# Upper weight parts of the first up projection: seven of eight made on GpSimd instead of ScalarE

## The chip, the cores and the metric

The kernel runs on one core of a Trainium2 chip. The metric is the device time of one execution in microseconds (us). The engines are named as the profile names them: PE is TensorE's matmul (PEld its weight load), DVE is VectorE, ACT is ScalarE, POOL is GpSimd and SP is SyncE, which issues the DMAs here.

## The reference

What is computed is chunked attention with memory tokens, followed by two feed-forward blocks, all in float32:

```python
# attention: 4 x 8 heads, 768 positions, head size 64; chunks of 32 see 16 to the left, 8 to the right, 8 memory keys
scores = scale * np.matmul(q_c, k_full.transpose(0, 1, 3, 2))
a = np.exp(scores - np.max(scores, axis=-1, keepdims=True))
a = a / (np.sum(a, axis=-1, keepdims=True) + 1e-09)
out[:, :, c_start:c_end] = np.matmul(a, v_full)
# x: 3072 tokens x 512
h = x @ w_in                          # w_in 512 x 2048
g = s * np.maximum(h, 0.0) ** 2 + b
x = g @ w_out                         # 2048 x 512
h = x @ w2_in
return (h - np.tanh(h)) @ w2_out
```

The weights arrive in double precision. Each float32 product is made on TensorE from a rounded upper part and a remainder of both factors: three matmuls, upper with upper, remainder with upper, upper with remainder (`three`, L226 to L229). The factor `s` is taken into the first up projection as the product of its weights with `root`, the square root of |s|.

## The kernel before, in words

The tokens are worked in units of 128 (attention) and blocks of 512 (products). The program is written in a fixed order, `manual_schedule`: every engine runs its instructions in the order in which the code emits them. For the first hundred microseconds this order is the table `START`, a list of tokens such as `i5 k0 h5 r6 o5`; each is a letter for a step and a number. Attention of the first units, the preparation of the first up projection's weights and its first tiles are interleaved there.

The weights of the first up projection come in eight pieces n = 0 to 7, each 128 partitions by 1024 values. A piece passes through these tokens:

- `ra`: a DMA of the piece (1 MB) into one of two places (`raw`, L519), issued on SP. Piece n + 2 uses the place of piece n, so its load waits until `l` of piece n has read it. The same places serve the first load for the second up projection (`wl1`).
- `z`: ACT makes the scaled float32 word of the upper half (`scaled`, L234).
- `i`: DVE shifts it in place (`shifted`, L240).
- `o`: DVE fills in the low bits, into `raw` (`filled_in_raw`, L250). It reads two tensors in SBUF.
- `h`: the product of the shifted word with `root`, rounded: the upper part, the first half of `w` (`w1_high`, L541). It reads what `i` made and needs nothing of `o`.
- `l`: DVE makes the remainder from the filled word, `root` and the upper part: the second half of `w` (`w1_low`, L545). It reads two tensors in SBUF.

Beside them stand, for attention unit u: `S` scores on PE, `M` mask and `R` maximum on DVE (L380, L390), `E` eight exponentials on ACT (L398), `D` division: POOL adds 1e-9 to the sums (L411), DVE takes the reciprocal (L412) and multiplies (L413), `T` transposes on PE (L429), `C` copies on ACT, `V` products with the values on PE (L466), `X` and `L` upper part and remainder of the result. For tile t of the up projection: `F` products on PE (L227 to L229), `r` the relu on ACT (L572), `Q` the square, on ACT or on DVE (L586, which reads the product from PSUM and the relu from SBUF), `k` and `K` sums of finished tiles on DVE (L598, two tensors in SBUF). Tiles 2n and 2n + 1 need piece n; three PSUM banks serve the tiles in turn, so that tile t + 3 waits until tile t has been read. `ws1` is the first scaled word for the second up projection, on ACT (L234, `zw`).

Of the kernel before, what the change touches and what calls it, by code (L numbers as in the profile page):

```python
# [98 lines left out]
VALUES_BETWEEN = {  # L99
    0, 2, 6, 8, 10, 11,  # L100
}
HIGH_ON_VECTOR = set()
COPY_ON_VECTOR = set()
PLAIN_EXPONENTIALS = set()

# [36 lines left out]
def tile_chunk_attention_two_ffn(  # L142
# [11 lines left out]
    nc = tc.nc  # L154
# [30 lines left out]
    def new(place, n, dt, name):  # L185
        assert n <= SIZE[place[0]], (place, n)
        if place[0] in "QSRYWV":
            assert place[0] in side["letters"], place
        pool = arena if place[0] in "EZ" else side["of"]
        return pool.tile([P, n], dt, tag=place, name=name)  # L190
# [342 lines left out]

    def w1_high(n):
        w1_w[n] = new(A_W[n], 2048, F32R, "w")
        if n in HIGH_ON_VECTOR:
            nc.vector.tensor_scalar(
                out=w1_w[n][:, 0:1024], in0=w1_z[n], scalar1=root[:, 0:1], scalar2=None, op0=ALU.mult
            )
        else:  # L540
            nc.scalar.activation(out=w1_w[n][:, 0:1024], in_=w1_z[n], func=AF.Copy, scale=root[:, 0:1])  # L541
# [399 lines left out]
    def p2_store_sums(n):  # L941
# [5 lines left out]
        "T": transposes, "C": copies, "V": values, "X": x_high, "L": x_low,  # L947
        "ra": w1_load, "z": w1_scaled, "i": lambda n: shifted(w1_z[n]),
        "o": w1_filled, "h": w1_high, "l": w1_low,
        "G": lambda t: up1_products(t, 0, HB),  # L950
        "F": lambda t: up1_products(t, HB if t < HALVED else 0),
# [266 lines left out]
    for s in range(NQ - 1):  # L1218
        q, p, r = quads2[s], quads2[s - 1] if s else None, quads2[s + 1]
        n, g = q.n, q.g  # L1220
# [202 lines left out]
```

## Time and profile before

| | us |
|---|---|
| median of 3 runs | 1028.87 (1028.59 to 1029.10) |
| the profiled execution, its own time | 1029.12 |
| its span, first to last instruction | 1027.3 |
| PE busy | 1015.4 (99%) |
| DVE busy | 788.6 (77%) |
| ACT busy | 573.2 (56%) |
| POOL busy | 11.3 (1%) |
| granted TensorE clock, mean of the core | 1.000 |

Nearly all of the span is matmuls: the chain of work that ended last is PE for 93%. The shares of DVE and ACT are averages over stages. In the first tenth of the span, where the change lies, both are busy nearly all the time; there the question is which of the engines waits for another, and by how much each piece of work is early.

### The profile page before, as it was taken

The numbers are of one execution on the slowest core, as the hardware profiler recorded it, in microseconds if no ns is written. First come the engines' busy times: TensorE is split into PE (matmuls) and PEld (weight loads), VectorE is DVE, ScalarE is ACT, GpSimd is POOL, SyncE is SP. The second block draws the span as 40 slices with busy tenths as digits, with TensorE's granted clock in tenths as the row PEclk, the third lists the DMA queues.
The fourth block names the chain that finished last, engine by engine and source line by source line (L and its number), as shares of the span: only waits on it lengthen the run. The fifth ranks groups of instructions, "written<-read, shape, count | busy, mean of one in ns | idle before, by whom it ended". The sixth has DMA issues, their size and how long they took to land.

```text
span 1027.3 us, 15607 instructions
## 1 busy us (share of the span) xinstructions
PE 1015.4 (99%) x6112; PEld 842.0 (82%) x6112; DVE 788.6 (77%) x970; ACT 573.2 (56%) x1055; POOL 11.3 (1%) x53
## 2 busy tenths in 40 slices
PE   7999999999999999999999999999999999999998
PEld 5888888888888888888888888888888888888887
DVE  7999446888677878898788788888888966767654
ACT  8999635666435575666555544455445554444432
POOL 1000000000000000000000000000000000000000
PEclk9999999999999999999999999999999999999999
DMA  9798558888889997796652265655569995555761
GB/s 348 295 330 335 243 220 324 327 334 301 325 322 376 387 336 256 259 337 192 209 196 82 113 247 210 238 215 216 226 260 357 364 328 180 200 205 213 256 248 63
DMA packets 78506, 268.94 MB, mean 262 GB/s; under 512 B 5728, under 2 KB 5984, under 8 KB 67168
## 3 DMA queue, kind: packets, MB, share of 16 engines
q1 hardware_dynamic: 78432, 267.94, 70.8%
q8 instruction: 48, 0.79, 0.3%
q14 instruction: 26, 0.21, 0.1%
HBM read 160.96 MB, written 106.95 MB: 261 GB/s over the span
## 4 chain that ended last, share of the span: by engine, by line
PE 93%; DVE 3%; ACT 2%; DMA 1%; issue 0%; SPq 0%; DVEq 0%; ACTq 0%
PE pb L227 30%; PE pb L229 29%; PE pb L228 29%; PE pb L466 2%; PE pb L357 1%; PE pb L429 1%; ACT sm L398 1%; DMA o<-ob 1%; DMA qk<-in_qk_dram 1%; DVE oa L1167 0%; DVE nmx L390 0%; DVE sm L380 0%; DVE oa L864 0%; ACT pt L437 0%; DVE ob L864 0%
## 5 line engine op out<-in xcount | busy, mean ns | idle before, releaser
L228 PE MATMUL pb<-ringhringl,whl 128*128 128x512 f32 (+1 forms) x680 | 262.9, 387 | 0.0
L227 PE MATMUL pb<-ringhringl,whl 128*128 128x512 f32 (+1 forms) x680 | 262.8, 387 | 0.0
L229 PE MATMUL pb<-ringhringl,whl 128*128 128x512 f32 (+1 forms) x680 | 262.8, 386 | 0.0
L738 ACT ACTIVATE ringhringl<-part 128x1024 fp32r<-128x1024 f32 x120 | 127.0, 1060 | 149.0 <-PE pb L229 146.1
L739 DVE TENSOR_TENSOR ringhringl<-part,ringhringl 128x1024 fp32r<-128x1024 f32 x120 | 146.8, 1223 | 73.3 <-ACT ringhringl L738 73.0
L227 PE MATMUL pb<-xh,w 128*128 128x512 f32 (+1 forms) x392 | 152.9, 390 | 0.3 <-DVE oa L586 0.3
L228 PE MATMUL pb<-xh,w 128*128 128x512 f32 (+1 forms) x392 | 151.0, 385 | 0.1
L229 PE MATMUL pb<-xl,w 128*128 128x512 f32 (+1 forms) x392 | 151.0, 385 | 0.0
L229 PEld LDWEIGHTS pb<-ringhringl,whl 128*128 128x128 f32 x680 | 127.7, 188 | 26.1
L228 PEld LDWEIGHTS pb<-ringhringl,whl 128*128 128x128 f32 x680 | 127.7, 188 | 25.9
L227 PEld LDWEIGHTS pb<-ringhringl,whl 128*128 128x128 f32 x680 | 127.7, 188 | 25.7
L572 ACT ACTIVATE r<-pb 128x512 f32<-128x512 f32 x96 | 56.6, 595 | 91.9 <-PE pb L229 90.1
L227 PE MATMUL pb<-x2hx2l,w 128*128 128x512 f32 x224 | 87.3, 390 | 0.2 <-ACT keep L1163 0.2
L227 PEld LDWEIGHTS pb<-xh,w 128*128 128x128 f32 x392 | 73.6, 188 | 16.6 <-DVE oa L586 1.0
L228 PE MATMUL pb<-x2hx2l,w 128*128 128x512 f32 x224 | 87.2, 389 | 0.0
L229 PE MATMUL pb<-x2hx2l,w 128*128 128x512 f32 x224 | 87.1, 389 | 0.0
L229 PEld LDWEIGHTS pb<-xl,w 128*128 128x128 f32 x392 | 73.7, 188 | 15.0
L228 PEld LDWEIGHTS pb<-xh,w 128*128 128x128 f32 x392 | 73.7, 188 | 14.4 <-DVE w L545 0.3
L586 DVE TENSOR_TENSOR oa<-pb,r 128x512 f32<-128x512 f32 x62 | 42.5, 688 | 49.3 <-ACT r L572 49.3
L733 ACT ACTIVATE ringhringl<-part,b_c 128x1024 fp32r<-128x1024 f32 x48 | 55.1, 1151 | 34.1 <-PE pb L229 32.3
L1175 ACT ACTIVATE pb<-oa 128x512 f32<-128x512 f32 x72 | 43.2, 600 | 55.3 <-DVE oa L1167 54.4
L398 ACT ACTIVATE sm<-sm,nmx 128x96 f32<-128x96 f32 x192 | 69.2, 369 | 3.5 <-DVE nmx L390 3.5
(131 smaller groups left out, 1382.0 us busy)
## 6 DMA issues: line engine op xcount, KB each, us to landing
part<-o SPq DMA_DIRECT2D x84, 512.0 KB, 4.9
part<-o SPq DMA_DIRECT2D x42, 1024.0 KB, 6.2
o<-ob SPq DMA_DIRECT2D x24, 1024.0 KB, 5.4
o<-oa SPq DMA_DIRECT2D x24, 1024.0 KB, 3.9
o<-oa SPq DMA_DIRECT2D x24, 768.0 KB, 5.4
o<-ob SPq DMA_DIRECT2D x24, 768.0 KB, 5.1
raw<-in_wi_dram SPq DMA_DIRECT2D x16, 1024.0 KB, 6.4
raw<-in_wo_dram SPq DMA_DIRECT2D x16, 1024.0 KB, 8.2
```

The source lines that it names most:

```text
L227: nc.tensor.matmul(acc, lhsT=whi, rhs=xhi, start=first, stop=False, skip_group_check=more)
L228: nc.tensor.matmul(acc, lhsT=wlo, rhs=xhi, start=False, stop=False, skip_group_check=more)
L229: nc.tensor.matmul(acc, lhsT=whi, rhs=xlo, start=False, stop=last, skip_group_check=more)
L357: nc.tensor.matmul(score_bank(u, g)[QE * e:QE * (e + 1), KE * (r0 + r):KE * (r0 + r + 1)], lhsT=tq[sl, r, QE * e:QE * (e + 1)], rhs=tk[sl, ...
L398: nc.scalar.activation(out=sm[:, h, :], in_=sm[:, h, :], func=AF.Exp, bias=nmx[:, h:h + 1], scale=1.0, **({"accum_out": sums[:, h:h + 1]} ...
L466: nc.tensor.matmul(value_bank(u)[64 * g:64 * g + 64, c0:c0 + QE], lhsT=tv[0:KE, e, 2 * r + g, :], rhs=pt[0:KE, e, 4 * g + r, :], start=Tru ...
L572: nc.scalar.activation(out=r, in_=up_ps[p], func=AF.Relu)
L586: nc.vector.tensor_tensor(out=o, in0=ps2, in1=r2, op=ALU.mult)
L733: nc.scalar.activation(out=xh, in_=src, func=AF.Identity, bias=self.bias)
L738: nc.scalar.activation(out=xh, in_=src, func=AF.Copy)
L739: nc.vector.tensor_tensor(out=xl, in0=src, in1=xh.bitcast(F32), op=ALU.subtract)
L1175: nc.scalar.activation(out=self.rs[o], in_=src, func=AF.Tanh)
```

## The change

The product of `w1_high` is made by POOL for the pieces 1 to 7. Piece 0 stays on ACT. The token order `START` is the same, and so is the rest of the program.

```diff
-HIGH_ON_VECTOR = set()
+HIGH_ON_POOL = {1, 2, 3, 4, 5, 6, 7}
...
     def w1_high(n):
         w1_w[n] = new(A_W[n], 2048, F32R, "w")
-        if n in HIGH_ON_VECTOR:
-            nc.vector.tensor_scalar(
+        if n in HIGH_ON_POOL:
+            nc.gpsimd.tensor_scalar(
                 out=w1_w[n][:, 0:1024], in0=w1_z[n], scalar1=root[:, 0:1], scalar2=None, op0=ALU.mult
             )
         else:
             nc.scalar.activation(out=w1_w[n][:, 0:1024], in_=w1_z[n], func=AF.Copy, scale=root[:, 0:1])
```

On POOL's row the seven products (L537) come between the additions of the divisions (L411), in the first hundred microseconds; the difference of the whole row from there on:

```order
 L223 TENSOR_SCALAR root<-sroot_103 128x1
 L224 TENSOR_TENSOR b_c<-qk,sign 128x1
-L411 TENSOR_SCALAR sums<-sums 128x8 x24
+L411 TENSOR_SCALAR sums<-sums 128x8 x5
+L537 TENSOR_SCALAR w<-z,root 128x1024 x2
+L411 TENSOR_SCALAR sums<-sums 128x8 x2
+L537 TENSOR_SCALAR w<-z,root 128x1024 x3
+L411 TENSOR_SCALAR sums<-sums 128x8 x2
+L537 TENSOR_SCALAR w<-z,root 128x1024 x2
+L411 TENSOR_SCALAR sums<-sums 128x8 x15
```

Before, POOL had only the additions, one for each division; now the products of pieces 1 and 2 stand ahead of the additions of D5 and D6, those of pieces 3, 4 and 5 ahead of D7 and D8, and those of pieces 6 and 7 ahead of D9 and the next.

On DVE's row nothing moves, but the remainders (L545) wait for another engine. The place is l4, i5, k0 (two rows), o5, l5, M10 and the reciprocal of D7, with the semaphores waited for in brackets. Before:

```order
 L545 SCALAR_TENSOR_TENSOR w<-raw,root,w 128x1024 [waits DVE_49]
 L240 TENSOR_SCALAR z<-z 128x1024 [waits Activation_49]
 L598 TENSOR_TENSOR ob<-oa 128x512
 L598 TENSOR_TENSOR ob<-oa,ob 128x512 [waits DVE_49]
 L250 SCALAR_TENSOR_TENSOR raw<-raw,z 128x1024 [waits DMAHW1_49]
 L545 SCALAR_TENSOR_TENSOR w<-raw,root,w 128x1024 [waits DVE_49,Activation_49]
 L380 SCALAR_TENSOR_TENSOR sm<-pb,mask_mid 128x768 [waits PE_49]
 L412 RECIPROCAL rs<-sums 128x8 [waits Pool_49]
```

and now:

```order
 L545 SCALAR_TENSOR_TENSOR w<-raw,root,w 128x1024 [waits DVE_49,Pool_49]
 L240 TENSOR_SCALAR z<-z 128x1024 [waits Activation_49]
 L598 TENSOR_TENSOR ob<-oa 128x512
 L598 TENSOR_TENSOR ob<-oa,ob 128x512 [waits DVE_49]
 L250 SCALAR_TENSOR_TENSOR raw<-raw,z 128x1024 [waits DMAHW1_49]
 L545 SCALAR_TENSOR_TENSOR w<-raw,root,w 128x1024 [waits DVE_49,Pool_49]
 L380 SCALAR_TENSOR_TENSOR sm<-pb,mask_mid 128x768 [waits PE_49]
 L412 RECIPROCAL rs<-sums 128x8 [waits Pool_49]
```

What moved is the producer alone: the remainder waits for POOL where it waited for ACT.

## Rows read from the trace of the kernel before

**Rows 1.** Stretches: us; PE, PEld, DVE, ACT, POOL busy (instructions); clock; DMA share; GB/s

```profile
30.50:83.00 52.50, 52.50 (x611) 43.56 (x608) 49.94 (x64) 52.14 (x162) 3.37 (x7) 1.00 0.88 322
83.00:100.00 17.00, 16.73 (x309) 14.05 (x309) 15.29 (x24) 15.80 (x52) 0.46 (x2) 1.00 0.85 332
100.00:1000.00 900.00, 899.58 (x4648) 744.85 (x4645) 686.81 (x833) 472.19 (x739) 2.31 (x10) 1.00 0.71 261
```

**Rows 2.** Line L541, ACT's eight products: ns shortest/median/longest, first and last start

```profile
L541 ACT ACTIVATE w<-z,root x8: 1147/1152/1177, 23.7 to 70.5; 128x1024 fp32r<-128x1024 f32 x8
```

**Rows 3.** Timeline of POOL (start us, us, ..., idle before and releaser)

```profile
40.98 0.23 POOL L411 TENSOR_SCALAR sums<-sums 128x8 f32<-128x8 f32 x1 [6.13 <-ACT sm L398]
50.91 0.89 POOL L411 TENSOR_SCALAR sums<-sums 128x8 f32<-128x8 f32 x1 [9.70 <-ACT sm L398]
60.48 1.00 POOL L411 TENSOR_SCALAR sums<-sums 128x8 f32<-128x8 f32 x1 [8.68 <-DVE rs L412]
```

**Rows 4.** Timeline of DVE at those three times

```profile
40.23 0.95 DVE L380 SCALAR_TENSOR_TENSOR sm<-pb,mask_mid 128x768 f32<-128x768 f32 x1
...
50.48 1.23 DVE L250 SCALAR_TENSOR_TENSOR raw<-raw,z 128x1024 int32<-128x1024 int32 x1
...
60.44 0.96 DVE L413 TENSOR_TENSOR sm<-sm,rs 128x768 f32<-128x768 f32 x1
```

**Rows 5.** Groups of POOL's instructions (busy us, mean ns of one, idle before)

```profile
L301 POOL MEMSET mask_mid<- 128x192 f32 x1 | 0.3, 258 | 0.0
...
L1410 POOL MEMSET const-float32-1.0<- 128x1 f32 x1 | 0.1, 107 | 0.0
```

**Rows 6.** Timeline of DVE: i1 and o1, i2 and o2

```profile
29.78 0.69 DVE L240 TENSOR_SCALAR z<-z 128x1024 int32<-128x1024 int32 x1
...
30.99 1.21 DVE L250 SCALAR_TENSOR_TENSOR raw<-raw,z 128x1024 int32<-128x1024 int32 x1
...
35.59 0.69 DVE L240 TENSOR_SCALAR z<-z 128x1024 int32<-128x1024 int32 x1 [1.12 <-ACT z L234]
...
36.80 1.22 DVE L250 SCALAR_TENSOR_TENSOR raw<-raw,z 128x1024 int32<-128x1024 int32 x1
```

**Rows 7.** Timeline of DVE: i5 and o5, i6 and k1, i7 and D9's reciprocal

```profile
54.88 0.69 DVE L240 TENSOR_SCALAR z<-z 128x1024 int32<-128x1024 int32 x1
...
56.81 1.22 DVE L250 SCALAR_TENSOR_TENSOR raw<-raw,z 128x1024 int32<-128x1024 int32 x1
...
64.71 0.68 DVE L240 TENSOR_SCALAR z<-z 128x1024 int32<-128x1024 int32 x1
...
65.91 0.68 DVE L598 TENSOR_TENSOR ob<-oa 128x512 f32<-128x512 f32 x1
...
69.83 0.68 DVE L240 TENSOR_SCALAR z<-z 128x1024 int32<-128x1024 int32 x1
70.43 0.19 DVE L412 RECIPROCAL rs<-sums 128x8 f32<-128x8 f32 x1
```

**Rows 8.** Timelines of DVE and PE: Q4, l6; F7's start, T7's start, F12's second matmul

```profile
51.62 0.68 DVE L586 TENSOR_TENSOR oa<-pb,r 128x512 f32<-128x512 f32 x1
...
71.53 1.28 DVE L545 SCALAR_TENSOR_TENSOR w<-raw,root,w 128x1024 fp32r<-128x1024 f32 x1
...
52.37 0.50 PE L227 MATMUL pb<-xh,w 128*128 128x512 f32 x1
...
61.52 0.26 PE L429 MATMUL pb<-ident,sm 64*96 64x64 f32 x2
...
74.93 0.40 PE L228 MATMUL pb<-xh,w 128*128 128x512 f32 x1
```

**Rows 9.** Timelines of SP, ACT and PE: wl1's load, ws1, V8

```profile
72.95 0.38 SPq L519 DMA_DIRECT2D raw<-in_wi_dram  x1
...
84.16 1.19 ACT L234 ACTIVATE zw<-raw 128x1024 f32<-128x1024 f32 x1 [1.14 <-DMA raw<-in_wi_dram]
...
85.88 0.28 PE L466 MATMUL pb<-pt,v 96*64 96x64 f32 x2 [0.27 <-ACT r L572]
```

## The prediction, made before the changed kernel ran

> **What bounds the kernel now.** I read the stretches first, then the timelines of the engines in the stretch that the change touches, and last how early each result is that PE takes there. In [rows 1] see that PE is the bound from 30.5 us on: it is busy for all 52.50 us up to 83, stands idle for 0.27 us up to 100 and for 0.42 us in the 900 us after that. The first product that moves starts near 30.5 us, so all idle time of PE that the change could take back is 0.69 us, under 0.07% of the time. In the same first stretch ACT is busy for 52.14 and DVE for 49.94 of 52.50 us. PE is thus not waiting, but two engines feed it that have next to no room. What they deliver late shows up as a wait on PE, at once where the result is only just in time.
>
> Three results are just in time or nearly so [rows 4, 8]. Q4 on DVE ends at 51.62 + 0.68 = 52.30 and frees the bank in which F7 starts at 52.37: 0.07 us to spare. D7's multiplication ends at 60.44 + 0.96 = 61.40 and T7 starts at 61.52: 0.12 us. Piece 6's remainder ends at 71.53 + 1.28 = 72.81 and F12's second matmul, the first that reads it, is at 74.93: 2.12 us.
>
> **What is removed.** Seven of the eight products leave ACT, 7 x 1.152 = 8.1 us [rows 2]. None of it lies on the chain of PE, which waits for nothing there. It is worth something in one place: DVE waits 1.12 us for ACT's word at i2 [rows 6], and ACT, without the product of piece 1, comes 1.15 us or more sooner. I credit DVE with 1.12 us there. After it DVE has next to no wait for ACT to lose; 0.69 us is all that PE could gain.
>
> **What is added.** Seven products of 128x1024 on POOL. The trace has no such operation. Its bounds: two memsets of one and of 192 elements differ by 258 - 107 = 151 ns [rows 5], 0.79 ns an element, and the smallest tensor-scalar of POOL takes 0.23 us [rows 3]; 0.23 + 1016 x 0.79 ns = 1.03 us. If reading and writing took turns, twice the slope, it would be 1.83 us. From below, DVE's 0.69 us for a tensor-scalar of this size [rows 6] is the end. I take 1.05 us, an estimate, since the memset is POOL's own; call it H.
>
> The length itself would be hidden: the remainder of a piece comes 1.2 us or more after its shift on DVE, and between them lies `o`. What counts is what POOL and DVE do to each other. In [rows 3] and [rows 4] see three additions of 128x8 on POOL. At 40.98, while DVE masks scores (one operand in PSUM, one in SBUF), the addition takes 0.23 us. At 50.91 and 60.48, while DVE runs an instruction with two operands in SBUF, it takes 0.89 and 1.00 us and ends at 51.80 and 61.48, just after DVE's at 51.71 and 61.40. So POOL is shut out while such an instruction runs. I take it that DVE is shut out likewise while POOL reads; no row shows that direction, since POOL's additions are too small.
>
> The Trainium skill, "SBUF — State Buffer", section "Who interferes with whom", states both directions: VectorE and GpSimd share a port pair as an exclusive lock held for a whole instruction, and VectorE takes it for two SBUF inputs or in a two-port mode. The trace agrees with the first direction by the 0.89 and 1.00 us above, and no row here shows the second.
>
> Now piece by piece, what DVE loses. POOL starts 0.15 us after the shift ends (an allowance) and holds DVE's next two-operand instruction until it is done:
> - h1: the shift ends at 29.78 + 0.69 = 30.47, o1 stood at 30.99 [rows 6], 0.52 later. Loss H + 0.15 - 0.52 = 0.68.
> - h2: the same gap, 36.28 to 36.80 [rows 6], 0.68; and D5's addition now stands behind h2 on POOL, which adds its 0.23 [rows 3]. Loss 0.91.
> - h3: one masking of 0.95 us [rows 4], of which some 0.8 counts, lies between shift and o3. Loss 0.40.
> - h4: o4 follows the shift at once, so POOL waits for DVE, and then runs beside Q4, R8 and Q5, which have at most one operand in SBUF. Loss 0.
> - h5: both sums of k0 and then o5, all with two operands, follow the shift, from 54.88 + 0.69 = 55.57 on [rows 7]. POOL gets in between them or after them; either way DVE stands still for the whole of it, in the second case because l5 needs the product. Loss 1.05.
> - h6: shift ends 65.39, k1 stood at 65.91 [rows 7]. Loss 0.68.
> - h7: it stands on POOL ahead of D9's addition, and D9's reciprocal follows i7 directly on DVE (70.43, while the shift ends at 70.51) [rows 7]. So DVE waits for 0.15 + 1.05 + 0.23 and about 0.1 of signals, 1.53, and loses the 0.08 overlap: 1.62.
>
> Queued behind DVE's stops are all its later steps; PE waits for them at the three places named. Up to Q4 the loss is 0.68 + 0.91 + 0.40 = 1.99, less the 1.12 credit 0.87; less 0.07 to spare, F7 is 0.80 late. Up to D7 it is 0.87 + 1.05 = 1.92; less 0.12, T7 is 1.80 late. Up to l6 it is 1.92 + 0.68 + 1.62 = 4.22; less 2.12, F12 is 2.10 late. These are not added: each is PE's lateness so far.
>
> One more chain follows [rows 9]. The end of l6 frees the place for the load wl1, issued at 72.95; ACT takes it at 84.16 after waiting 1.14 us for the DMA, and behind it on ACT stands the relu for which PE waits 0.27 us at 85.88. So that chain is at its limit today. With l6 4.22 us later PE would be up to 4.22 us late; if the load lands sooner after its issue, for the transfers around it are then spread out, nothing is added to the 2.10. I take the middle, a little over 3. PE has no idle time later to make it up [rows 1]. All else that moves (ACT's other steps, about 1.15 us earlier each time) finds PE or a load late and is worth nothing.
>
> **Sum:** +3.0 us. From the profiled execution's own 1029.12 this gives 1032.1; the median of the runs shown is 0.25 lower, and from it the forecast is 1028.87 + 3.0 = 1031.9.
>
> **The rivals.**
>
> *Nothing that counts.* If POOL does not shut DVE out, or only for a short part of its instruction, only h7's wait ahead of D9 and D5's addition are left. 1.62 + 0.23 - 1.12 = 0.7 us of lateness at l6 is inside the 2.12 to spare, and PE is late by nothing, or by 0.5 us if part of h5 remains. The same comes of a product as short as DVE's 0.69: the loss up to l6 is six times H less 0.96 and less 1.12, so 2.1 us, just what there is to spare, and T7 is 0.4 late. Time: 1028.6 to 1029.9. For it: nothing in the trace shows DVE held by POOL. Against it: POOL is held to the end of DVE's instruction both times [rows 3, 4].
>
> *A long product.* At twice the slope, 1.83 us, the loss up to l6 is 6 x 1.83 - 2.08 = 8.9 us. T7 is then 4.9 late, F12 6.8, and the load chain up to 8.9: 1028.87 + 6.8 to 8.9, 1035.7 to 1037.8. For it: the multiplication by a value for each partition and the rounding of the result are more work than a memset. Against it: the small tensor-scalars cost only 0.23 us.
>
> The Trainium skill, "GPSIMD Engine Reference", section "3.1 Elementwise — side-by-side cycle accounting", gives 769 ns for 512 elements as its best case of a loop; doubled to 1.54 us, an estimate, the loss up to l6 would be 7.2 us. Its section "4.1 Engine selection" calls one-input work about line rate. No run here shows either yet.
>
> *Faster.* ACT is relieved of 8.1 us and PE catches what it waits for after 83 us. The most that this gives is 0.69 us [rows 1], 1028.2; it is decided by whether DVE loses less than ACT's credit, that is, the sum above falls under 1.12. That ACT were the hidden limit of PE elsewhere is spoken against by PE's 52.50 busy of 52.50.
>
> That the change does not do what it says can be left out: the order shows the products on POOL's row.
>
> **How the numbers follow.** The forecast, DVE shut out by a product near 1.05 us, +2.1 to +4.2 us: 45%. A longer product, +4.2 to +9: 17%. Nothing that counts, 0 to +1.5: 33%. Faster, to -0.7: 5%. About 0.2%, 2.06 us, is what a measurement of this kernel can tell from no change. The forecast lies nearly all above it, the long product wholly, the rival of nothing hardly: slower 60%. Faster by over 0.2% would need three times PE's idle time: 3%. The rest, 37%, is within 0.2%. For the range I take in nothing that counts and most of the long product, 1028.6 to 1036.5, leaving out gains beyond 0.3 us and the longest products. The likeliest case alone would be 1031.0 to 1033.1.
>
> **What would show it.** In the changed kernel the products (L537) take 1.0 to 1.2 us where DVE runs single-operand work, and longer, up to DVE's end, at piece 4. o1, o2 and k1 (L250, L598) start or end 0.4 to 0.9 us later behind the shift than before, and D9's reciprocal 1.6 us later. PE shows waits for DVE at F7, T7 and F12, 2 us in sum, in a stretch that had none, and one for ACT's relu near 88 us. DVE's instructions with two operands would read longer than 1.22 us where they stand behind POOL. I am wrong if these keep their length and places: then POOL does not hold DVE. I am wrong in size if L537 takes 1.5 us or more, and wrong in the end of the chain if wl1's load still lands 11 us after its issue, or if F12's lateness is made up behind it.

## The result, and the profile after

| | before | changed |
|---|---|---|
| median of 5 runs, us | 1028.87 | 1037.70 (1037.25 to 1038.43) |
| ratio | | 1.0086 (95% interval 1.0075 to 1.0097) |
| span of the profiled execution, us | 1027.3 | 1035.5 |
| ACT busy, us | 573.2 | 566.5 |
| POOL busy, us | 11.3 | 32.0 |

The changed kernel is slower by 8.8 us, 0.86%. The forecast was slower by 3.0 us, with a range up to 1036.5. The direction came true; the size did not, and the time lies outside the range.

The stretches of the changed kernel, in the columns of [rows 1]:

```profile
30.50:83.00 52.50, 46.07 (x573) 37.74 (x573) 45.73 (x54) 38.95 (x129) 23.33 (x12) 0.99 0.81 295
83.00:100.00 17.00, 17.00 (x236) 14.03 (x236) 14.28 (x23) 13.36 (x47) 0.91 (x3) 0.93 0.72 269
100.00:1000.00 900.00, 899.58 (x4718) 744.72 (x4715) 690.41 (x841) 477.20 (x763) 2.54 (x11) 1.00 0.70 261
```

Against [rows 1]: PE, which was busy for all 52.50 us of the first stretch, now stands idle for 6.43 of them. ACT's busy time fell from 52.14 to 38.95 us, but DVE's fell too, from 49.94 to 45.73: it waits. The clock of PE is below 1.00 for a while. From 100 us on PE is as busy as before, 899.58 us, at the full clock.

POOL's timeline in the changed kernel (start us, us, ..., idle before and releaser):

```profile
30.50 2.85 POOL L537 TENSOR_SCALAR w<-z,root 128x1024 fp32r<-128x1024 f32 x1 [2.02 <-DVE z L240]
36.24 2.85 POOL L537 TENSOR_SCALAR w<-z,root 128x1024 fp32r<-128x1024 f32 x1 [2.88 <-DVE z L240]
39.17 0.56 POOL L411 TENSOR_SCALAR sums<-sums 128x8 f32<-128x8 f32 x2
45.37 2.85 POOL L537 TENSOR_SCALAR w<-z,root 128x1024 fp32r<-128x1024 f32 x1 [5.65 <-DVE z L240]
52.57 3.87 POOL L537 TENSOR_SCALAR w<-z,root 128x1024 fp32r<-128x1024 f32 x1 [4.34 <-DVE z L240]
58.46 3.22 POOL L537 TENSOR_SCALAR w<-z,root 128x1024 fp32r<-128x1024 f32 x1 [2.02 <-DVE z L240]
...
74.56 2.84 POOL L537 TENSOR_SCALAR w<-z,root 128x1024 fp32r<-128x1024 f32 x1 [2.82 <-DVE z L240]
77.49 0.24 POOL L411 TENSOR_SCALAR sums<-sums 128x8 f32<-128x8 f32 x1
```

A product takes 2.85 us, not the 1.05 us that I took, and not the 1.83 us of my upper bound either. At piece 4 it takes 3.87 us: it is issued at 52.57, just after DVE has begun o4, and first waits for that instruction, as predicted. The last two rows are the dearest: D9's addition stands behind h7 and comes when h7 is done.

DVE's timeline in the changed kernel, the instructions that are longer or wait:

```profile
30.92 1.78 DVE L250 SCALAR_TENSOR_TENSOR raw<-raw,z 128x1024 int32<-128x1024 int32 x1
33.39 1.28 DVE L545 SCALAR_TENSOR_TENSOR w<-raw,root,w 128x1024 fp32r<-128x1024 f32 x1 [0.69 <-POOL w L537]
...
36.65 1.77 DVE L250 SCALAR_TENSOR_TENSOR raw<-raw,z 128x1024 int32<-128x1024 int32 x1
39.44 0.20 DVE L412 RECIPROCAL rs<-sums 128x8 f32<-128x8 f32 x1 [1.02 <-POOL sums L411]
...
46.05 1.51 DVE L250 SCALAR_TENSOR_TENSOR raw<-raw,z 128x1024 int32<-128x1024 int32 x1
48.26 1.28 DVE L545 SCALAR_TENSOR_TENSOR w<-raw,root,w 128x1024 fp32r<-128x1024 f32 x1 [0.70 <-POOL w L537]
...
56.48 1.28 DVE L545 SCALAR_TENSOR_TENSOR w<-raw,root,w 128x1024 fp32r<-128x1024 f32 x1 [0.69 <-POOL w L537]
...
59.00 1.49 DVE L598 TENSOR_TENSOR ob<-oa,ob 128x512 f32<-128x512 f32 x1
...
69.30 1.24 DVE L598 TENSOR_TENSOR ob<-oa 128x512 f32<-128x512 f32 x1
...
73.78 0.69 DVE L240 TENSOR_SCALAR z<-z 128x1024 int32<-128x1024 int32 x1
77.76 0.20 DVE L412 RECIPROCAL rs<-sums 128x8 f32<-128x8 f32 x1 [3.30 <-POOL sums L411]
```

There are two kinds. Five instructions with two operands in SBUF (o1, o2, o3, the second sum of k0 and the first of k1) are longer than in the kernel before: by 0.57, 0.55, 0.29, 0.80 and 0.56 us, 2.8 us in sum. And DVE stands in front of POOL's results: 0.69, 0.70 and 0.69 us at l1, l3 and l4, 1.02 at D5 and 3.30 at D9, 6.4 us in sum. The second kind is more than twice the first.

PE's timeline in the changed kernel, the first rows of F7, T7, T9 and the start of F12, with the masking M12 on DVE that T9 waits for:

```profile
54.38 0.50 PE L227 MATMUL pb<-xh,w 128*128 128x512 f32 x1 [0.75 <-DVE oa L586]
...
65.06 0.26 PE L429 MATMUL pb<-ident,sm 64*96 64x64 f32 x2 [0.94 <-DVE sm L413]
...
80.07 0.95 DVE L380 SCALAR_TENSOR_TENSOR sm<-pb,mask_first 128x768 f32<-128x768 f32 x1
81.07 0.32 PE L429 MATMUL pb<-ident,sm 64*96 64x64 f32 x4 [3.67 <-DVE sm L380]
...
82.00 0.63 PE L228 MATMUL pb<-xh,w 128*128 128x512 f32 x1
82.42 0.63 PE L229 MATMUL pb<-xl,w 128*128 128x512 f32 x1
```

M12 and T9 in the kernel before:

```profile
72.73 0.95 DVE L380 SCALAR_TENSOR_TENSOR sm<-pb,mask_first 128x768 f32<-128x768 f32 x1
...
74.01 0.65 PE L429 MATMUL pb<-ident,sm 64*96 64x64 f32 x16
```

F7 starts at 54.38 instead of 52.37, T7 at 65.06 instead of 61.52 [rows 8]. T9 waits 3.67 us for a masking (L380, M12), which empties the bank that T9 writes. Before, M12 ended at 73.68, 0.33 us ahead of T9; now it comes 7.34 us later, and T9 7.06 us. Then the matmuls of F12 start 0.42 us apart instead of 0.23. The granted clock in three stretches of 4 us of the changed kernel tells why (columns as in [rows 1]):

```profile
78.00:82.00 4.00, 0.93 (x18) 0.81 (x18) 4.00 (x4) 1.76 (x6) 0.00 (x0) 1.00 0.70 239
82.00:86.00 4.00, 4.00 (x12) 3.15 (x11) 3.97 (x6) 1.88 (x11) 0.00 (x0) 0.58 0.87 295
86.00:90.00 4.00, 4.00 (x20) 3.27 (x19) 3.67 (x8) 4.00 (x13) 0.46 (x2) 1.00 1.01 416
```

PE is busy for 0.93 of the 4 us up to 82, and in the next stretch its granted clock is 0.58, near the lower level of 1.2 GHz; then 2.4 GHz again. F12's first matmul comes 7.07 us later than before, F13's 8.66: so the slow clock took 1.6 us.

### The profile page after: what moved, and what is told of

It reads as the page before. It is cut to its first block, busy times and chain, and to the rows that moved or that the text cites. A ratio compares the mean times of both kernels' runs of the same rounds, so it can differ in the third digit from the quotient of the medians.

```text
span 1035.5 us, 15622 instructions
## 1 busy us (share of the span) xinstructions
PE 1017.6 (98%) x6112; PEld 842.9 (81%) x6112; DVE 791.3 (76%) x970; ACT 566.5 (55%) x1048; POOL 32.0 (3%) x60
## 4 chain that ended last, share of the span: by engine, by line
PE 88%; DVE 2%; ACT 1%; DMA 1%; issue 0%; DVEq 0%; ACTq 0%
PE pb L227 29%; PE pb L228 28%; PE pb L229 28%; PE pb L466 1%; PE pb L429 1%; PE pb L357 1%; DMA o<-ob 1%; DVE oa L1167 0%; DVE oa L864 0%; ACT sm L398 0%; DVE ob L864 0%; DVE ob L598 0%; DVE x2hx2l L864 0%; ACT pb L1175 0%; DVE w L864 0%
```

## The experiments

Theory A: DVE loses most where it waits for the end of a long product. Theory B, on which most terms of the forecast rested: DVE is shut out by a product for its whole length. The first four of these kernels and their runs of the kernel before (median 1029.04) come from one chip. The changed kernel's 1037.70 was measured beside a median of 1028.87, 0.17 us lower.

**Piece 7 back on ACT.**

```diff
-HIGH_ON_POOL = {1, 2, 3, 4, 5, 6, 7}
+HIGH_ON_POOL = {1, 2, 3, 4, 5, 6}
```

> Pieces 1 to 6 on POOL, piece 7 back on ACT. Theory A, DVE loses most where it has to wait for the end of a long product: in the changed kernel D9's reciprocal waits 3.3 us for the addition that stands behind h7 on POOL. Without h7 that wait goes, PE keeps the 3.5 us of lateness that it has at T7, and its granted clock stays at 1.00 up to 100 us: 1032.0 to 1033.0 us. Theory B, DVE is shut out by every product for its whole length, so each counts about alike: one seventh of 8.8 us is saved, 1036.0 to 1037.0 us.

Measured: 1032.89 us, ratio 1.0033 (1.0021 to 1.0046). The stretches of this kernel:

```profile
30.50:83.00 52.50, 49.61 (x600) 40.51 (x596) 49.00 (x59) 41.77 (x141) 21.52 (x11) 1.00 0.84 301
83.00:100.00 17.00, 17.00 (x271) 14.19 (x270) 15.15 (x25) 16.11 (x58) 1.14 (x4) 1.00 0.83 312
```

One product of seven, with what it holds up, makes up more than half of the loss, 1037.70 - 1032.89 = 4.8 of 8.8 us, and in these stretches the clock stays at 1.00. Theory A holds here.

**Piece 7 alone on POOL.**

```diff
-HIGH_ON_POOL = {1, 2, 3, 4, 5, 6, 7}
+HIGH_ON_POOL = {7}
```

> Piece 7 alone on POOL. Theory A: D9's reciprocal waits about 3.3 us, the masking M12 behind it on DVE is as late, and T9 on PE, which had 0.33 us to spare for it, waits some 3 us: 1031.9 us, and up to 1033.5 us if PE's granted clock falls after that idle time as it did in the changed kernel between 83 and 100 us. Theory B: one seventh of 8.8 us, 1030.1 us.

Measured: 1032.98 us (1031.23 to 1034.47), ratio 1.0033 (1.002 to 1.0046). DVE's timeline of this kernel, then its stretches around the wait (PE, PEld, DVE, ACT, POOL, clock, DMA, GB/s):

```profile
69.75 0.68 DVE L240 TENSOR_SCALAR z<-z 128x1024 int32<-128x1024 int32 x1
73.73 0.20 DVE L412 RECIPROCAL rs<-sums 128x8 f32<-128x8 f32 x1 [3.30 <-POOL sums L411]
```

```profile
74.00:78.00 4.00, 0.95 (x17) 0.83 (x18) 4.00 (x4) 2.17 (x8) 0.00 (x0) 0.94 0.87 289
78.00:82.00 4.00, 4.00 (x12) 3.14 (x12) 3.97 (x6) 1.90 (x11) 0.00 (x0) 0.63 0.92 276
```

DVE is on time up to i7 (69.83 in [rows 7]) and then waits 3.30 us. PE is idle behind it, and its clock falls to 0.63. In the median of five runs the product alone costs 3.9 us, wait and clock together. By the mean clock of each run the fall does not come every time: two of the five runs have one of 1.000 and took 1031.23 and 1031.50 us, 2.2 and 2.5 us over the kernel before; the other three have 0.996 to 0.998 and took 1032.98 to 1034.47 us. The trace is of one of these three. By these two kernels pieces 1 to 6 and piece 7 cost about the same, 3.85 and 3.94 us over the kernel before; they do not quite add up to the 8.8 us.

**All seven on POOL, two additions put ahead.** POOL's addition becomes a token of its own, `a`, ahead of h2 and of h7.

```diff
-... i2 F2 h2 E6 Q0 ... o2 D5 l2 ...
+... i2 F2 a5 h2 E6 Q0 ... o2 D5 l2 ...
-... F10 i7 h7 D9 T8 ...
+... F10 i7 a9 h7 D9 T8 ...
```

> All seven products on POOL, with the additions of D5 and D9 put ahead of h2 and h7 on POOL. Theory A: DVE's waits of 1.0 us at D5 and 3.3 us at D9 go; what is left on DVE is three waits of 0.7 us at l1, l3 and l4 and 2.8 us of lengthened instructions, less the 1.1 us that ACT gives back; PE some 2.5 to 3 us late at T7 and no later behind it, clock 1.00: 1031.3 to 1032.3 us. Theory B: the products are as long and shut out DVE as long, 1036.5 to 1037.7 us.

Measured: 1032.06 us, ratio 1.0028 (1.0018 to 1.0039). POOL's timeline of this kernel around piece 7, and DVE's:

```profile
70.42 1.27 POOL L412 TENSOR_SCALAR sums<-sums 128x8 f32<-128x8 f32 x1
73.16 3.64 POOL L544 TENSOR_SCALAR w<-z,root 128x1024 fp32r<-128x1024 f32 x1 [1.47 <-DVE z L240]
```

```profile
72.38 0.68 DVE L240 TENSOR_SCALAR z<-z 128x1024 int32<-128x1024 int32 x1
72.98 0.19 DVE L419 RECIPROCAL rs<-sums 128x8 f32<-128x8 f32 x1
...
74.08 2.06 DVE L552 SCALAR_TENSOR_TENSOR w<-raw,root,w 128x1024 fp32r<-128x1024 f32 x1
```

The products are the same seven, and 5.6 us of the loss are gone with two additions of 0.23 us moved past them: the two waits, and with the long one the fall of the clock. The reciprocal follows the shift at once again. The new row to see is the last: D9's multiplication now holds up h7 (3.64 us instead of 2.85), which then shuts out l6 for 0.78 us. M12 behind it is late by that, and T9 still waits 1.04 us for it in this kernel's trace; the expectation had PE no later behind T7.

**Products that nobody waits for.** ACT makes all upper parts; POOL makes the seven products a second time into an idle place, with the additions ahead.

```diff
         if n in HIGH_ON_POOL:
+            nc.scalar.activation(out=w1_w[n][:, 0:1024], in_=w1_z[n], func=AF.Copy, scale=root[:, 0:1])
             nc.gpsimd.tensor_scalar(
-                out=w1_w[n][:, 0:1024], in0=w1_z[n], ...
+                out=new("Z11", 1024, F32R, "idle"), in0=w1_z[n], ...
```

> As with the additions ahead, but ACT makes all upper parts as before, and POOL makes the same seven products once more into a place that nobody reads, so that nothing waits for them; the result is the reference's. What is left is what the products do to DVE's own instructions. Theory A: the two-operand instructions behind the shifts are longer by 0.3 to 0.8 us each as in the changed kernel, 2.8 us in sum, of which the 1.1 us that DVE waits for ACT at i2 covers the first; PE about 1.5 us late at T7 and 1.9 at T9: 1030.3 to 1031.0 us. Theory B, shut out is the whole loss: 1036 us or more.

Measured: 1031.24 us (1030.62 to 1031.50), ratio 1.0018 (1.0009 to 1.0027). Three of DVE's rows, o1, o2 and l6:

```profile
31.20 1.78 DVE L250 SCALAR_TENSOR_TENSOR raw<-raw,z 128x1024 int32<-128x1024 int32 x1
...
37.02 1.85 DVE L250 SCALAR_TENSOR_TENSOR raw<-raw,z 128x1024 int32<-128x1024 int32 x1
...
73.61 2.14 DVE L553 SCALAR_TENSOR_TENSOR w<-raw,root,w 128x1024 fp32r<-128x1024 f32 x1
```

Being shut out is real, and by itself it costs 2.2 us. That is 0.2 us above theory A's interval; what l6 loses behind h7, 0.78 us above and 2.14 - 1.28 = 0.86 us here, was not in its sum. Against the kernel with the additions ahead, whose DVE waits 2.1 us for products at l1, l3 and l4, this one is only 1032.06 - 1031.24 = 0.8 us faster. In part that is because it lacks ACT's relief: its DVE still waits 0.56 us for ACT at i2. What covers the rest is not shown.

**What a product costs.** Idle products of several forms, ACT making all upper parts, with the additions ahead.

```diff
+            nc.scalar.activation(out=w1_w[n][:, 0:1024], ...
+            size, dt, by = {1: (1024, F32R, 1), 2: (1024, F32, 1), 3: (512, F32R, 1), 4: (1024, F32, 1),
+                            5: (512, F32, 1), 6: (1024, F32, 0), 7: (1024, F32R, 0)}[n]
             nc.gpsimd.tensor_scalar(
-                out=w1_w[n][:, 0:1024], in0=w1_z[n], ...
+                out=new("Z11", size, dt, "idle"), in0=w1_z[n][:, 0:size],
+                scalar1=root[:, 0:1] if by else 1.5, scalar2=None, op0=ALU.mult,
```

> ACT makes all upper parts; POOL makes idle products of several forms, to price them: piece 1 as in the change (1024 values, rounded fp32r output, factor for each partition), 2 and 4 with plain f32 output, 3 with 512 values and fp32r, 5 with 512 and f32, 6 with 1024, f32 and a constant factor, 7 with 1024, fp32r and a constant factor. Theory R, the rounded output is a second pass: 2.85 us at piece 1, near 1.05 us at 2 and 6, 1.4 us at 3. Theory S, POOL's loop costs about 2.6 ns a value whatever the output: 2.85 us at 1, 2, 6 and 7, and 1.5 us at 3 and 5. Under both, DVE's two-operand instruction behind the shift is held until about 1.0 us after the product's start for 1024 values, and less for 512.

The one execution timed took 1030.29 us. Its time decides nothing; its rows do. POOL's timeline of this kernel, then DVE's:

```profile
30.79 2.85 POOL L547 TENSOR_SCALAR idle<-z,root 128x1024 fp32r<-128x1024 f32 x1 [2.02 <-DVE z L240]
...
36.66 2.85 POOL L547 TENSOR_SCALAR idle<-z,root 128x1024 f32<-128x1024 f32 x1 [1.51 <-DVE z L240]
...
44.75 1.57 POOL L547 TENSOR_SCALAR idle<-z,root 128x512 fp32r<-128x512 f32 x1 [3.32 <-DVE z L240]
...
66.15 2.78 POOL L547 TENSOR_SCALAR idle<-z 128x1024 f32<-128x1024 f32 x1 [4.95 <-DVE z L240]
```

```profile
31.21 1.77 DVE L250 SCALAR_TENSOR_TENSOR raw<-raw,z 128x1024 int32<-128x1024 int32 x1
33.10 1.28 DVE L556 SCALAR_TENSOR_TENSOR w<-raw,root,w 128x1024 fp32r<-128x1024 f32 x1
...
45.37 1.22 DVE L250 SCALAR_TENSOR_TENSOR raw<-raw,z 128x1024 int32<-128x1024 int32 x1
...
56.65 1.06 DVE L609 TENSOR_TENSOR ob<-oa,ob 128x512 f32<-128x512 f32 x1
```

The rounding costs nothing, 2.85 us with and without it, and a constant factor saves 0.07. Half the values take 1.57 us: (2.85 - 1.57) / 512 = 2.5 ns a value and 0.29 us besides. Theory S holds, theory R falls.

See in DVE's rows how long a product shuts it out. The first ends at 32.98; with its usual 1.22 us it started in earnest at 31.76, 0.97 us after the product did. The second (l1) runs from 33.10 in its usual 1.28 us while the product goes on to 33.64. So only the first third of the product keeps DVE's two-operand instructions out. With 512 values the third, 0.62 us behind the product's start, is not held at all, and the fourth, caught at the start of one, is 0.37 us longer instead of 0.80: (0.80 - 0.37) / 512, about 0.8 ns a value.

**A product with room on both sides.** Piece 6 alone on POOL.

```diff
-HIGH_ON_POOL = {1, 2, 3, 4, 5, 6, 7}
+HIGH_ON_POOL = {6}
```

> Piece 6 alone on POOL. Theory A (a wait for the product's end costs, being shut out costs only the first 1.0 us of the product): the product of 2.85 us ends before anything asks for it; only the sum k1 on DVE is 0.56 us later, of which PE has 0.33 us to spare at T9: 1028.9 to 1029.4 us, the same as before. Theory B, shut out for the whole product: k1 2.4 us later, T9 2.0 us: 1030.9 us, and more if the clock falls.

Measured: 1029.28 us against 1028.98 of the kernel before on the same chip, ratio 1.0003 (0.9994 to 1.0012). POOL's timeline and DVE's of this kernel:

```profile
65.71 2.85 POOL L537 TENSOR_SCALAR w<-z,root 128x1024 fp32r<-128x1024 f32 x1 [4.00 <-DVE z L240]
```

```profile
66.13 1.24 DVE L598 TENSOR_TENSOR ob<-oa 128x512 f32<-128x512 f32 x1
67.40 0.69 DVE L598 TENSOR_TENSOR ob<-oa,ob 128x512 f32<-128x512 f32 x1
```

A product of 2.85 us can lie there for nothing: nobody asks for it before its end, and DVE loses only 0.56 us at k1. It gains nothing either. None of the kernels is faster than the kernel before, and by [rows 1] none with this change could be by more than 0.69 us.

## Why the prediction was right or wrong, point by point

- **What bounds the kernel: right.** PE had nothing to win back, and the results of DVE that were just in time were where the loss appeared: the waits at F7 and T7 are in the rows above.
- **ACT's relief: right.** The 1.12 us that DVE waited for ACT at i2 are gone in the changed kernel: i2 starts at 35.45 us, 35.59 before, though l1 ahead of it came later.
- **The length of a product: wrong, and the step that failed.** I took 1.05 us from the slope of a memset, 0.79 ns a value, and 1.83 us as the upper end; it is 2.85 us. The trace before held no compute instruction of POOL with more than 8 values in a row besides the making of `ident` (128x128, 0.28 us), so no row could bound it from above. "The length itself would be hidden" fell with it: at l1, l3 and l4 DVE waits 0.69 to 0.70 us for the product, and h4, for which I put down 0, costs 0.69.
- **DVE is shut out while POOL works: right in kind and in size, for a wrong reason.** I put DVE's instruction back by the whole product, H = 1.05 us from its start; measured is 0.97 us from its start. What I took for the whole product is its first third. So h1's loss by shutting out, 0.68 in the sum, is 0.57, h6's 0.68 is 0.56, h5's 1.05 is 0.80 and h3's 0.40 is 0.29. The rival of a long product multiplied both with H and would have been wrong the other way: at 2.85 us its formula gives 6 x 2.85 - 2.08 = 15 us at l6, and D9's reciprocal, with l6 behind it, is 7.4 us late (77.76 against 70.43 in [rows 7], 0.07 us allowed for the earlier start). The Trainium skill, "SBUF — State Buffer", section "Who interferes with whom", has the pair locked for a whole instruction; the second direction, which no row before showed, is now shown by the 1.78 us of o1, but the 1.28 us of l1 beside the rest of an idle product (33.10 to 34.38, the product going on to 33.64) speaks against "whole", and the measurement decides.
- **h7 ahead of D9's addition: right mechanism, mis-sized term.** It was the largest single term with 1.62 us. It is 3.98 us from the shift's start to the reciprocal instead of 0.60, 3.4 us in all, with H = 2.85 in the place of 1.05. The kernel with the two additions ahead shows that this queue, with D5's and with the slow clock behind it, carries 5.6 of the 8.8 us.
- **The places where PE waits: two of three.** F7 and T7 came as named, 2.0 and 3.5 us late instead of 0.80 and 1.80. The third was not F12 but T9: it writes a bank that the masking M12 on DVE has to empty first, and M12 comes right behind l6. The prediction followed D9 on DVE as far as its reciprocal and l6, and not the bank; T9 and M12 do not stand in it.
- **The clock: missed.** The forecast had PE late but always at full clock, and no term for it in the sum. In the changed kernel a wait of 3.67 us was followed by 1.6 us of loss at the lower level, with piece 7 alone a wait of 3.24 us by 1.5 us, and none of the traces without the long wait shows such a loss there. With piece 7 alone two of five runs, with a mean clock of 1.000, did not have it; why is open.
- **The load chain behind l6: wrong, but small.** wl1's load and ws1 are late, yet PE waits for no relu there any more, as it is later itself. The middle of 2.10 and 4.22 us that I took for it, about 1 us, belongs at nothing. The profile shows PE 8.66 us late at F13 and 8.2 at the end of the span: about 0.4 us is made up, 0.27 us of it by the relu's wait of before [rows 9], which is gone.
- **The rivals.** "Nothing that counts" falls by the kernel with idle products, 2.2 us from shutting out alone. Its condition, that DVE is held for a short part of the product only, is half true, but the part is 0.97 us, nearly the whole H of the forecast. "A long product" was the right one in its main point, the length, and I gave it 17%. That the measured 1037.70 lies in its 1035.7 to 1037.8 is luck: it was worked out for 1.83 us, with DVE held all the while and without T9's bank and the clock. Its reasons fell too: the rounding costs nothing, the value for each partition 0.07 us.

What stays open is how the other losses share out exactly: piece 7 alone and pieces 1 to 6 together account for 7.8 of 8.8 us, the rest being within what the intervals of these kernels leave.

## What to carry to other kernels

Where the order of work has been tuned until no engine waits, a piece of work moved to an idle engine is paid at three places: what it takes there, what it holds up on an engine that it shuts out, and what stands behind it in the new queue; here the last was the largest, above all a 0.23 us addition behind a 2.85 us product. Price a move by an instruction of the same kind on the new engine, or by one idle copy of it in a kernel on the chip, before anything else is worked out. And ask for each result on time not only who makes it, but also who has to empty the place that it goes to.

## What the runs showed of the hardware that was not expected

- POOL's tensor-scalar in f32 costs 2.5 ns a value and 0.29 us besides (2.85 us for 128x1024, 1.57 us for 128x512), whether the result is rounded to fp32r or not. ACT takes 1.15 us for the same product [rows 2], DVE 0.69 us for an integer shift of the same size [rows 6].
- Only about the first 0.97 us of the 2.85 us keep DVE's two-operand instructions out, 0.8 ns a value; later ones run beside the rest at their usual length. The other way round POOL waits out nearly the whole of DVE's instruction: 3.87 us instead of 2.85 behind o4, of which 1.16 us were left when the product was issued.
- In the traces of two kernels a wait of PE of 3.67 and 3.24 us was followed by a stretch of 4 us with a granted clock of 0.58 and 0.63; waits of up to 0.94 us in the changed kernel and 1.04 us with the additions ahead were followed by none. Two runs of the kernel with piece 7 alone kept a mean clock of 1.000.
